# An mLSTM cell with a feed-forward block: loading the second chunk's output gates later and applying them in a step of their own

## The chip, the cores and the metric

The kernel runs on one core of a Trainium2 chip. The metric is the device time of one launch in microseconds (us). The core has five engines with a queue each: TensorE for matrix products (PE; its weight loads are shown as PEld), VectorE (DVE), ScalarE (ACT), GpSimd (POOL), and SyncE (SP), which here only issues loads and stores (DMAs). Each engine works through its own instructions in program order and waits on semaphores for what the others make.

## The reference

Two blocks follow one another. The first is an mLSTM cell with 4 batch rows, 8 heads, 768 steps and 40 numbers a head; the second is a feed-forward block with 2048 hidden features on the 3072 x 320 result.

```python
def _attn_ref(q, k, v, i_gate, f_gate, o_gate):
    ...
    for t in range(S):
        ...
        m_new = np.maximum(f_gate[:, :, t] + m, i_gate[:, :, t])
        f_stab = np.exp(f_gate[:, :, t] + m - m_new)
        i_stab = np.exp(i_gate[:, :, t] - m_new)
        m = m_new
        C = f_stab[:, :, None, None] * C + i_stab[:, :, None, None] * np.einsum('bhd,bhe->bhde', vt, kt)
        n = f_stab[:, :, None] * n + i_stab[:, :, None] * kt
        h_tilde = np.einsum('bhde,bhe->bhd', C, qt)
        nq = np.einsum('bhd,bhd->bh', n, qt)[:, :, None]
        denom = np.maximum(np.abs(nq), 1.0)
        o = 1.0 / (1.0 + np.exp(-o_gate[:, :, t]))
        y[:, :, t] = o * h_tilde / denom

def _moe_ref(x, w_in, w_out):
    h = x @ w_in
    g = h * np.cos(h)
    return g @ w_out
```

What matters here is the last line of the cell: an output is the value h_tilde, divided by denom and multiplied by the gate o. The two factors may be applied in either order and at different times, as long as both are in x before `x @ w_in` reads it.

## The kernel before, in words

**Cells and chunks.** The 768 steps are cut into 6 chunks of 128 steps. A cell is one chunk of one batch row, so there are 24 cells, numbered `n = 4 * chunk + row` from 0. A cell's product of scores and values is made by PE, normalised and gated, and written, turned so that features lie on partitions, into the tile `xT[chunk]`. This tile holds three blocks of features (two of 128, and one of 64 that is kept twice) for all 4 rows.

**The feed-forward slots.** Once the four cells of a chunk are in xT, their 512 tokens go through the feed-forward block in 8 slots, called `f2` from 0 to 7, with two 128-wide tiles of hidden features in each. `Up(c, f2)` issues the products with w_in into two banks of PSUM: eight matmuls on the two whole blocks (line 810) and four on the block of 64 (line 816). Then `near` (ACT, 824), `rest` (DVE, 827), `sin` (ACT, 832) and `gate` (DVE, 836) make h * cos(h). The pool `ps_u` has just the two banks of one Up, so the next Up starts only when the gates of the one before it have been made. `down(c, f2)` multiplies by w_out (848).

**What runs beside what.** `first_cells` makes cells 0 to 3. While chunk 0 goes through its slots, `first_parts(b)`, called for b = 0 to 3, makes cell `4 + b` of chunk 1 between the instructions of slots `2b` (i = 0) and `2b + 1` (i = 1). `both_parts` does the same for the later chunks. All is under a manual schedule: the order in the program is the order in every engine's queue. In `first_parts` the down product runs one slot behind, so that Up(0,7) is followed by down(0,6), then by Up(1,0), which is the first to read the xT of chunk 1.

**Weights.** w_in and w_out come in a 64-bit form. A piece is loaded into a tile `bits`, `take_apart` (two ACT instructions, lines 158 and 160) and `put_together` (three DVE instructions, 165 to 169, and one of POOL, 170) turn it into float32. w_in comes in four groups of three pieces, each group for two slots; the pool `pb` has four such tiles. w_out comes in eight pieces, one for each slot; `pc` has three tiles. `more` issues the next w_in piece's loads when a tile comes free, `next_out` does it for w_out.

**Output gates.** `load_o(c)` issues eight loads on SP into one raw tile. `sigmoid(c)` is three ACT instructions into `og`, of which there is one. ACT needs a table load (1.28 us each in this profile) when it changes between exponential, sigmoid and sine; `sin_next` loads the sine's table ahead of its use. For the cells of chunk 1, `turn_gate(n)` has DVE transpose a cell's gates into `oT` (line 524), and `normalize_turned(n)` makes 1/denom in `dt`, multiplies the values by the gates into `yt` (664), spreads 1/denom into `db` (668), and writes two blocks of xT (672). POOL makes the third block in `yt` (673), and `low_out(n)` has POOL issue two copies of it into xT (776). The pool `p1`, where oT, yt, db and the scaled queries qG lie, has one buffer for each tag: whoever writes such a tile next waits until all readers of the last content are done.

**Other names in the steps.** `scores`, `weigh`, `values` are a cell's products and the weighing by the decay E; `decay_exponents` masks E on POOL (438) and `decay` is its exponential on ACT (452). `turn_keys`/`keys_out` transpose keys on PE (502) and copy them by ACT (510), `turn_blocks` transposes queries on DVE (519), `scale_q` scales them on POOL (528), `seam_u`, `fade` and `state` carry the state. `hold(9)` issues nine dummy matmuls (1029).

Of the kernel before, what the change touches and what calls it, by code (L numbers as in the profile page):

```python
# [29 lines left out]
def kernel(  # L30
# [144 lines left out]
    def weights_in(f):  # L175
        for i in range(NK):
            src = [(slice(32 * a, 32 * a + 32), w_in_bits[D * (NK * a + i):D * (NK * a + i) + 32, ts(f, WP)]) for a in range(HP)]
            yield w_in_sb[:, i, ts(f, WP)], bits_in(WP, src, pb, WP)
        bits = pb.tile([128, WP, 2], I32, name="bits", tag="bits")
        for e in range(2):  # L180
            for a in range(2):
                nc.sync.dma_start(out=bits[64 * e:64 * e + 64, ts(a, 128)].rearrange("r n two -> r (n two)"), in_=w_in_last[e, 2 * f + a])
        yield w_in_l[:, ts(f, 2)].rearrange("p a n -> p (a n)"), bits
# [146 lines left out]
    def load_o(c, bs=range(B)):  # L330
        if c == 0:
            sig[c] = og.rearrange("q b k i -> q (b k i)")[:, 0:B * DM].rearrange("q (b h d) -> q b h d", b=B, h=H)
            for b in bs:
                nc.sync.dma_start(out=sig[c][:, b], in_=o_gate[b, :, ts(c, C)].rearrange("h t d -> t h d"))  # L334
            return
        raw_o[c] = p1.tile([128, B, 2 * C // 32, D], FP, name="o", tag="o")
        src = o_gate.rearrange("b (a g) (c t k) d -> a g c t b (k d)", g=2, k=C // 32, t=32)
        for a in range(HP):
            for g in range(2):
                dst = raw_o[c][32 * a:32 * a + 32].rearrange("t b (g k) d -> t g b (k d)", g=2)[:, g]  # L340
                nc.sync.dma_start(out=dst, in_=src[a, g, c])
# [306 lines left out]
    def normalize_turned(n):  # L648
# [24 lines left out]
        nc.gpsimd.tensor_tensor(out=yt[:, NK], in0=yt[:, NK], in1=db[:, NK], op=OP.mult)  # L673
        ys[n] = yt[:, NK]

    def normalize(n):
        c, b = divmod(n, B)
        hs = heads_of[n]
        dn = p2.tile([128, H], FP, name="dn", tag="dn")

        nc.vector.scalar_tensor_tensor(out=dn, in0=hs[:, :, D], scalar=-TWO_PI, in1=least, op0=OP.mult, op1=OP.max)
        nc.vector.scalar_tensor_tensor(out=dn, in0=hs[:, :, D], scalar=TWO_PI, in1=dn, op0=OP.mult, op1=OP.max)
        nc.vector.reciprocal(out=dn, in_=dn)
        y = p1.tile([128, 3 * C], FP, name="y", tag="yt")[:, 0:DM]
        t = p1.tile([128, 3 * C], FP, name="yo", tag="db")[:, 0:DM].rearrange("q (h d) -> q h d", h=H)
# [345 lines left out]
    def first_cells():  # L1031
# [68 lines left out]
        seam_out(0)  # L1100
        values(1)
        load_E(B + 1)
        load_o(1)
        scores(2)
        decay_exponents(3)
        normalize(1)
# [64 lines left out]
    def more():  # L1171
        for piece in feed[0]:
            pieces.append(piece)
            break

    def first_parts(b):
        n = B + b
        for i in range(2):
            f2 = 2 * b + i
            up = Up(0, f2)  # L1180
            if (b, i) == (0, 0):
                feed.append(piece for f in range(2, NF // 4) for piece in weights_in(f))
                more()
                load_E(n + 2)
                outs.append((2, weights_out(2)))
            if i == 0:
                scores(n)
                if b == 0:
                    seam_u(B - 1)
                    warm(3, psum_o())  # L1190
# [5 lines left out]
                if b > 0:  # L1196
# [6 lines left out]
                if b == 0:  # L1203
                    state(B - 1)
                    for e in range(2):
                        up.gate(e)
                    turn_blocks(n + 1)
                    next_out()
                    decay_exponents(n + 1)
                    sigmoid(1)  # L1210
                else:
                    for step in "gw" if b == 1 else "wg":
                        if step == "g":
                            for e in range(2):
                                up.gate(e)
                        elif pieces:
                            put_together(*pieces.pop(0))
                            more()
                    next_out()
                    decay(n + 1)  # L1220
                down_slot(0, f2)
                turn_gate(n)
                values(n)
                seam_u(n)
                fade(n)
                normalize_turned(n)
                low_out(n)
                if n == 2 * B - 1:
                    load_two(n + 3, "qk")
                if n > B + 1:  # L1230
                    load_E(n + 3)
                if b == B - 2:
                    load_o(2)
                sin_next()
                if b > 0:
                    if pieces:
                        take_apart(*pieces[0])
                        put_together(*pieces.pop(0))
                        more()
                        take_apart(*pieces[0])  # L1240
                    take_apart(*outs[0][1])
            else:
                if n == 2 * B - 1:
                    load_two(n + 3, "Kv")
                for e in range(2):
                    up.near(e)
                if b == 0:
                    for piece in pieces[0:2]:
                        take_apart(*piece)
                    put_together(*pieces.pop(0))  # L1250
                    more()
                for e in range(2):
                    up.rest(e)
                if b == 0:
                    put_together(*pieces.pop(0))
                    more()
                    load_two(n + 2, "Kv")
                else:
                    state(n)
# [6 lines left out]
                if b == 0:  # L1266
                    take_apart(*pieces[0])
                    take_apart(*outs[0][1])
                if b == 0:
                    state(n)  # L1270
                if pieces:
                    put_together(*pieces.pop(0))
                    if b == 0:
                        load_two(n + 2, "q")
                    more()
                if n == B + 1:
                    low_dimensions(n + 1)
                if b == 0:
                    decay(n + 1)
                else:  # L1280
                    turn_blocks(n + 1)
                    if b < B - 1:
                        turn_keys(n + 1)
                        keys_out(n + 1)
                next_out()
                scale_q(n + 1)
                down_slot(0, f2)
                if b == 0:
                    turn_keys(n + 1)
                    keys_out(n + 1)  # L1290
                    hold(9)
                if b == 1:
                    load_two(n + 3)
                if b < 2:
                    load_E(n + 3)
                if b == 1:
                    take_apart(*pieces[0])
                if b == B - 1:
                    weight_sums(0)

    def both_parts(c, b):
# [120 lines left out]
```

## Time and profile before

| | |
|---|---|
| median of 3 runs | 518.31 us (517.14 to 519.41) |
| the profiled execution's own time | 517.64 us |
| its span on the core | 515.9 us |
| first Up, Up(0,0), starts | 35.87 us |
| Up(0,2) starts | 59.34 us |
| Up(0,6) starts | 104.94 us |
| Up(1,0) starts | 126.10 us |
| granted TensorE clock | 1.00 throughout |

The page lists each engine's busy time. A timeline lists an engine's instructions in order: start and duration in us, engine, source line, operation, tile written and tiles read, and in brackets how long the engine was idle before it, and who released it. A wait list says which line waited for whom: us in total, how many times, the longest. In the listing of DMAs, "to landing" is the time from issue to arrival.

Over the 64 us from 66 to 130, PE is busy 63.27, DVE 55.38, ACT 46.38 and POOL 32.72 us, and the mean share of the 16 DMA engines is full; from 130 us on it is 0.32. In the 25 us from 35 to 60, PE is busy 21.98 us, the dummy matmuls among them.

### The profile page before, as it was taken

The numbers are of one execution on the slowest core, as the hardware profiler recorded it, in microseconds if no ns is written. First come the engines' busy times: TensorE is split into PE (matmuls) and PEld (weight loads), VectorE is DVE, ScalarE is ACT, GpSimd is POOL, SyncE is SP. The second block draws the span as 40 slices with busy tenths as digits, with TensorE's granted clock in tenths as the row PEclk, the third lists the DMA queues.
The fourth block names the chain that finished last, engine by engine and source line by source line (L and its number), as shares of the span: only waits on it lengthen the run. The fifth ranks groups of instructions, "written<-read, shape, count | busy, mean of one in ns | idle before, by whom it ended". The sixth has DMA issues, their size and how long they took to land.

```text
span 515.9 us, 13717 instructions
## 1 busy us (share of the span) xinstructions
PE 504.5 (98%) x5271; PEld 336.3 (65%) x5271; DVE 411.4 (80%) x965; ACT 316.1 (61%) x696; POOL 266.6 (52%) x434
## 2 busy tenths in 40 slices
PE   9999799999999999999999999999999999999996
PEld 5764455565576675775775775776776676666766
DVE  6687988987779888898878898878898778664636
ACT  4879897955876765965764965765854631323221
POOL 7627555644677778566455366455365333131211
PEclk9999999999999999999999999999999999999999
DMA  9997999999166466019574019475020000010001
GB/s 135 221 226 195 231 204 261 204 217 199 20 149 109 89 134 113 5 59 183 113 143 99 3 61 184 111 136 102 10 73 11 2 7 8 1 52 0 2 0 51
DMA packets 97265, 53.17 MB, mean 103 GB/s; under 512 B 62544, under 2 KB 89280, under 8 KB 97200
## 3 DMA queue, kind: packets, MB, share of 16 engines
q1 hardware_dynamic: 95408, 50.46, 47.7%
q0 software_dynamic: 1408, 1.48, 1.1%
q8 instruction: 41, 0.67, 0.6%
q10 hardware_dynamic: 384, 0.36, 0.2%
q14 instruction: 24, 0.20, 0.1%
HBM read 46.86 MB, written 4.11 MB: 99 GB/s over the span
## 4 chain that ended last, share of the span: by engine, by line
PE 80%; SPq 6%; ACT 5%; DVE 3%; DMA 3%; issue 2%; POOL 1%; ACTq 0%; DVEq 0%; POOLq 0%
PE pup L810 30%; PE acc L931 24%; PE pup L816 9%; PE po L848 4%; PE late L931 4%; PE vt L619 2%; SPq L359 2%; PE vt L630 2%; PE ps L550 2%; ACT E L452 1%; DMA bits<-in_moe_w_out_dram 1%; DVE n L827 1%; PE ps L554 1%; DMA G<-G_d 1%; SPq L334 1%
## 5 line engine op out<-in xcount | busy, mean ns | idle before, releaser
L810 PE MATMUL pup<-xT,w_in_sb 128*128 128x512 f32 x384 | 175.5, 600 | 2.1 <-DVE g L836 1.9
L824 ACT ACTIVATE n<-pup 128x512 int32<-128x512 f32 x96 | 53.7, 593 | 156.3 <-PE pup L816 100.9
L810 PEld LDWEIGHTS pup<-xT,w_in_sb 128*128 128x128 f32 x384 | 69.7, 190 | 87.9 <-issue 80.7
L827 DVE SCALAR_TENSOR_TENSOR n<-pup,n 128x512 f32<-128x512 f32 x96 | 63.3, 687 | 72.8 <-ACT n L824 70.7
L890 POOL TENSOR_TENSOR D<-g 128x128 f32<-128x128 f32 x40 | 20.0, 499 | 110.1 <-DVE g L836 103.0
L832 ACT ACTIVATE n<-n 128x512 f32<-128x512 f32 x96 | 59.3, 630 | 13.6 <-DVE n L827 13.6
L836 DVE SCALAR_TENSOR_TENSOR g<-pup,n 128x512 f32<-128x512 f32 x96 | 63.2, 686 | 3.1 <-ACT n L832 0.2
L931 PE MATMUL acc<-w_out_sb,g 128*128 128x160 f32 x320 | 58.5, 304 | 0.0
L931 PE MATMUL acc<-T,g 128*128 128x160 f32 x320 | 57.9, 301 | 0.1
L816 PE MATMUL pup<-xT,w_in_l 64*128 64x512 f32 x192 | 54.5, 642 | 0.1
L931 PEld LDWEIGHTS acc<-w_out_sb,g 128*128 128x128 f32 x320 | 47.8, 190 | 4.6 <-issue 3.7
L931 PEld LDWEIGHTS acc<-T,g 128*128 128x128 f32 x320 | 48.1, 190 | 3.2 <-issue 2.7
L452 ACT ACTIVATE E<-E,tab 128x64 f32<-128x64 f32 (+1 forms) x160 | 42.1, 345 | 1.3 <-POOL E L438 1.0
L848 PE MATMUL po<-w_out_sb,g 128*128 128x320 f32 x128 | 36.4, 437 | 0.4 <-POOL w_out_sb L170 0.4
L673 POOL TENSOR_TENSOR yt<-yt,db 128x128 f32<-128x128 f32 x20 | 11.0, 552 | 49.2 <-DVE db L668 49.2
L931 PE MATMUL acc<-T,S 128*128 128x160 f32 x160 | 34.9, 300 | 0.0
L528 POOL TENSOR_TENSOR qG<-t,G 128x512 f32<-128x512 f32 x20 | 25.4, 1272 | 12.4 <-DVE t L519 10.4
L848 PEld LDWEIGHTS po<-w_out_sb,g 128*128 128x128 f32 x128 | 23.7, 190 | 11.3 <-issue 1.5
L816 PEld LDWEIGHTS pup<-xT,w_in_l 64*128 64x128 f32 x192 | 14.7, 184 | 24.0 <-issue 20.6
L438 POOL TENSOR_SCALAR_AFFINE_SELECT E<-E 64x512 f32<-64x512 f32 (+1 forms) x38 | 27.5, 724 | 3.0 <-DVE E L435 1.9
L931 PE MATMUL acc<-w_out_sb,S 128*128 128x160 f32 x160 | 28.8, 299 | 0.0
L931 PEld LDWEIGHTS acc<-T,S 128*128 128x128 f32 x160 | 26.2, 190 | 2.7 <-issue 2.7
(214 smaller groups left out, 960.1 us busy)
## 6 DMA issues: line engine op xcount, KB each, us to landing
qr<-in_q_dram SPq DMA_DIRECT2D x36, 160.0 KB
G<-G_d SPq DMA_DIRECT2D x20, 256.0 KB
bits<-in_moe_w_out_dram SPq DMA_DIRECT2D x8, 640.0 KB
kr<-in_k_dram SPq DMA_DIRECT2D x32, 160.0 KB
bits<-in_moe_w_in_dram SPq DMA_DIRECT2D x32, 128.0 KB
E<-M_d SPq DMA_DIRECT2D x32, 128.0 KB
out_dram<-o_sb SPq DMA_DIRECT2D x22, 160.0 KB
o<-in_o_gate_dram SPq DMA_DIRECT2D x40, 80.0 KB
```

The lines of the kernel that those rows point to most:

```text
L438: nc.gpsimd.affine_select(out=E[x:x + w], in_=E[x:x + w], compare_op=OP.is_ge, fill=1.0e30, base=0, pattern=[[0, H], [1, w]], channel_mult ...
L452: nc.scalar.activation(out=Es[n][:, h], in_=Es[n][:, h], func=AF.Exp, scale=-1.0, bias=tab[:, c, 0, g:g + 1])
L528: nc.gpsimd.tensor_tensor(out=qG, in0=qkT[n][0], in1=Gs[n], op=OP.mult)
L810: nc.tensor.matmul(pu, w_in_sb[:, i, ts(2 * f2 + e, 128)], x(i), start=(i == 0 and not low_first), stop=(i == NK - 1 and low_first))
L816: nc.tensor.matmul(pu, w_in_l[r, f2], x(NK, r), start=low_first, stop=not low_first)
L824: nc.scalar.activation(out=self.n[e], in_=self.pu[e], func=AF.Copy, bias=0.25)
L827: nc.vector.scalar_tensor_tensor(out=self.n[e].bitcast(FP), in0=self.pu[e], scalar=0.25, in1=self.n[e], op0=OP.add, op1=OP.subtract)
L832: nc.scalar.activation(out=r, in_=r, func=AF.Sin, scale=TWO_PI_DOWN)
L836: nc.vector.scalar_tensor_tensor(out=g, in0=self.pu[e], scalar=TWO_PI, in1=self.n[e].bitcast(FP), op0=OP.mult, op1=OP.mult)
L848: nc.tensor.matmul(po[c][b], gs[c, f][:, ts(b, C)], w_out_sb[:, f], start=(f == 0), stop=(f == NF - 1))
L890: tt(out=D1, in0=G0[:, 1, 1], in1=G1[:, 1, 1], op=OP.add)
L931: nc.tensor.matmul(a, lhs, rhs, start=start, stop=stop)
```

## The change

It has three parts. `load_o(1)` moves from `first_cells`, where it stood ahead of w_in's second group on SP, to the end of b = 0, behind the loads of later weights, keys and queries and behind load_E(7). `sigmoid(1)` moves from b = 0 to b = 2, and `load_o(2)` stays behind it. As the gates of chunk 1 come later, cells 4, 5 and 6 are normalised without them by `normalize_first`, and gated later by `gate_late`, in b = 3: cell 4 before the gates of Up(0,6), cell 5 after down(0,5) has been issued, cell 6 at the end of the last slot's work. Cell 7 is made as before. Last, the work of b = 0 is written out in `first_slots` in another order: keys of cell 5 are turned after Up(0,2) has been issued (in b = 1, i = 0), all three pieces of w_in's second group are taken apart before `near` of Up(0,1), and the dummy matmuls are left out.

```diff
+    def normalize_first(n):
+        c, b = divmod(n, B)
+        dn = p2.tile([128, C], FP, name="dt", tag="dt")
+        va, vb = heads_of[n]
+        nc.vector.tensor_scalar(out=dn, in0=va[:, 1], scalar1=-TWO_PI, scalar2=TWO_PI, op0=OP.mult, op1=OP.max)
+        nc.vector.scalar_tensor_tensor(out=dn, in0=va[:, 1], scalar=TWO_PI, in1=dn, op0=OP.mult, op1=OP.max)
+        nc.vector.reciprocal(out=dn, in_=dn)
+        db = p1.tile([128, 3, C], FP, name="db", tag="db")
+        for i, mask in enumerate(([FROM0] * 32, [FROM1] * 32, [FROM0] * 16 + [FROM1] * 16)):
+            nc.vector.stream_shuffle(out=db[:, i], in_=dn, mask=mask)
+        if b == 0:
+            xT[c] = p2.tile([128, NK + 1, B, C], FP, name="xT", tag="xT")
+        nc.vector.tensor_tensor(out=xT[c][:, 0:3:2, b], in0=va, in1=db[:, 0:3:2], op=OP.mult)
+        nc.vector.tensor_tensor(out=xT[c][:, 1, b], in0=vb, in1=db[:, 1], op=OP.mult)
+
+    def gate_late(n):
+        c, b = divmod(n, B)
+        turn_gate(n)
+        yt = p1.tile([128, 3, C], FP, name="yt", tag="yt")
+        nc.gpsimd.tensor_tensor(out=yt[:, NK], in0=xT[c][:, NK, b], in1=oTs[n][:, NK], op=OP.mult)
+        ys[n] = yt[:, NK]
+        low_out(n)
+        nc.gpsimd.tensor_tensor(out=xT[c][:, 0:NK, b], in0=xT[c][:, 0:NK, b], in1=oTs[n][:, 0:NK], op=OP.mult)
...
         load_E(B + 1)
-        load_o(1)
         scores(2)
...
+    def first_slots():
+        n = B
+        up = Up(0, 0)
...
+        take_apart(*outs[0][1])
+        state(B - 1)
+        for e in range(2):
+            up.gate(e)
+        turn_blocks(n + 1)
+        next_out()
+        decay_exponents(n + 1)
+        for piece in pieces[0:2]:
+            take_apart(*piece)
+        join()
+        values(n)
+        seam_u(n)
+        fade(n)
+        join()
+        up = Up(0, 1)
+        take_apart(*pieces[0])
+        for e in range(2):
+            up.near(e)
+        for e in range(2):
+            up.rest(e)
+        join()
+        for e in range(2):
+            up.sin(e)
+            up.gate(e)
+        load_two(n + 2, "Kv")
+        load_two(n + 2, "q")
+        take_apart(*outs[0][1])
+        weigh_k(n + 1)
+        odd_values(n + 1)
+        scale_q(n + 1)
+        decay(n + 1)
+        normalize_first(n)
+        next_out()
+        state(n)
+        down_slot(0, 1)
+        load_E(n + 3)
+        load_o(1)
...
             if i == 0:
+                if b == 1:
+                    turn_keys(n)
+                    keys_out(n)
                 scores(n)
...
+                if b < B - 1:
+                    decay_exponents(n + 1)
+                else:
+                    gate_late(B)
                     decay_exponents(n + 1)
...
-                    decay_exponents(n + 1)
-                    sigmoid(1)
...
                 down_slot(0, f2)
-                turn_gate(n)
+                if b == B - 1:
+                    gate_late(B + 1)
+                    turn_gate(n)
                 values(n)
                 seam_u(n)
                 fade(n)
-                normalize_turned(n)
-                low_out(n)
+                if b == B - 1:
+                    normalize_turned(n)
+                    low_out(n)
+                else:
+                    normalize_first(n)
...
                 if b == B - 2:
+                    sigmoid(1)
                     load_o(2)
...
-                if b == 0:
-                    turn_keys(n + 1)
-                    keys_out(n + 1)
-                    hold(9)
...
                 if b == B - 1:
+                    gate_late(B + 2)
                     weight_sums(0)
```

`join` is `put_together` of the first waiting w_in piece, followed by `more`. `B` is 4, `NK` is 2.

More of the change, by code (lines that the diff above doesn't have):

```diff
@@ L1174, in more, with join @@
             break
+    def join():
+        if pieces:
+            put_together(*pieces.pop(0))
+            more()
+    def first_slots():
+        n = B
+        up = Up(0, 0)
+        feed.append(piece for f in range(2, NF // 4) for piece in weights_in(f))
+        more()
+        load_E(n + 2)
+        outs.append((2, weights_out(2)))
+        scores(n)
+        seam_u(B - 1)
+        warm(3, psum_o())
+        for e in range(2):
+            up.near(e)
+        for e in range(2):
+            up.rest(e)
+        weigh(n)
+        for e in range(2):
[16 more added lines that the diff above has]
+        take_apart(*pieces[0])
+        for e in range(2):
+            up.near(e)
+        for e in range(2):
+            up.rest(e)
+        join()
+        for e in range(2):
+            up.sin(e)
+            up.gate(e)
[12 more added lines that the diff above has]
+        load_o(1)
     def first_parts(b):
         n = B + b
+        if b == 0:
+            first_slots()
+            return
         for i in range(2):
@@ L1180, in first_parts @@
             up = Up(0, f2)
[L1181 to L1185, printed above, removed]
             if i == 0:
+                if b == 1:
+                    turn_keys(n)
+                    keys_out(n)
                 scores(n)
-                if b == 0:
-                    seam_u(B - 1)
-                    warm(3, psum_o())
                 for e in range(2):
@@ L1195, in first_parts @@
                 weigh(n)
-                if b > 0:
+                if b < B - 1:
+                    decay_exponents(n + 1)
+                else:
+                    gate_late(B)
                     decay_exponents(n + 1)
@@ L1202, in first_parts @@
                 take_apart(*outs[0][1])
[L1203 to L1208, printed above, removed]
-                    decay_exponents(n + 1)
-                    sigmoid(1)
[L1211 to L1220, printed above, removed]
+                for step in "gw" if b == 1 else "wg":
+                    if step == "g":
+                        for e in range(2):
+                            up.gate(e)
+                    else:
+                        join()
+                next_out()
+                decay(n + 1)
                 down_slot(0, f2)
-                turn_gate(n)
+                if b == B - 1:
+                    gate_late(B + 1)
+                    turn_gate(n)
                 values(n)
@@ L1225, in first_parts @@
                 fade(n)
-                normalize_turned(n)
-                low_out(n)
+                if b == B - 1:
+                    normalize_turned(n)
+                    low_out(n)
+                else:
+                    normalize_first(n)
                 if n == 2 * B - 1:
@@ L1232, in first_parts @@
                 if b == B - 2:
+                    sigmoid(1)
                     load_o(2)
                 sin_next()
[L1235 to L1241, printed above, removed]
+                if pieces:
+                    take_apart(*pieces[0])
+                    join()
+                    take_apart(*pieces[0])
+                take_apart(*outs[0][1])
             else:
@@ L1246, in first_parts @@
                     up.near(e)
[L1247 to L1251, printed above, removed]
                 for e in range(2):
                     up.rest(e)
[L1254 to L1259, printed above, removed]
+                state(n)
                 for e in range(2):
@@ L1265, in first_parts @@
                 odd_values(n + 1)
[L1266 to L1276, printed above, removed]
-                    low_dimensions(n + 1)
[L1278 to L1282, printed above, removed]
-                        turn_keys(n + 1)
-                        keys_out(n + 1)
+                join()
+                if b == 1:
+                    low_dimensions(n + 1)
+                turn_blocks(n + 1)
+                if b < B - 1:
+                    turn_keys(n + 1)
+                    keys_out(n + 1)
                 next_out()
@@ L1287, in first_parts @@
                 down_slot(0, f2)
-                if b == 0:
-                    turn_keys(n + 1)
-                    keys_out(n + 1)
-                    hold(9)
                 if b == 1:
                     load_two(n + 3)
-                if b < 2:
                     load_E(n + 3)
-                if b == 1:
                     take_apart(*pieces[0])
                 if b == B - 1:
+                    gate_late(B + 2)
                     weight_sums(0)
```

## The prediction

> **What bounds the kernel now.** First the page's busy shares, then the waits of PE after 130 us:
>
> ```profile
> PE 504.5 (98%) x5271; PEld 336.3 (65%) x5271; DVE 411.4 (80%) x965; ACT 316.1 (61%) x696; POOL 266.6 (52%) x434
> ```
>
> ```profile
> PE pup L810 <- DVE g L836: 0.2, 1, 0.2
> ```
>
> TensorE (PE) sets the end. From 130 us to the end it waited for other engines 0.2 us in all, so nothing there can absorb a delay, and what PE loses or wins earlier moves the end one for one. What it can win lies in the first slots. SP's timeline, then PE's (start, duration, line; idle before it and its releaser in brackets):
>
> ```profile
> 34.58 9.86 SPq L341 DMA_DIRECT2D o<-in_o_gate_dram  x8
> 44.61 4.87 SPq L147 DMA_DIRECT2D bits<-in_moe_w_in_dram  x8
> 49.58 2.65 SPq L182 DMA_DIRECT2D bits<-in_moe_w_in_dram  x4
> 52.27 0.45 SPq L364 DMA_DIRECT2D ks<-in_k_dram  x1
> ```
>
> ```profile
> 50.57 4.57 PE L848 MATMUL po<-w_out_sb,g 128*128 128x320 f32 x16
> 56.07 0.63 PE L502 MATMUL pt<-ident,ks 128*128 128x128 f32 x4 [0.92 <-DMA ks<-in_k_dram]
> 56.54 1.40 PE L1029 MATMUL po<-nil 128*128 128x320 bf16 x9
> 59.34 3.67 PE L810 MATMUL pup<-xT,w_in_sb 128*128 128x512 f32 x8 [1.40 <-DVE g L836]
> ```
>
> The eight o_gate loads hold SP's queue for 9.86 us; w_in's second group stands behind them. PE ends its first down product at 55.05 and starts Up(0,2) at 59.34. Between lie the keys' load, nine dummy matmuls and the gates of Up(0,1), which on VectorE (DVE) stand behind the late weights. Those 4.29 us are all that the head can give; two later waits of PE, 0.33 and 0.40 us at 82 and 88 us, are the only other ones before 130.
>
> **Where the change puts a wait.** The seam to the second chunk: PE's, DVE's and GpSimd's (POOL's) timelines, then the landing of the copy that low_out(7) issues.
>
> ```profile
> 121.69 4.58 PE L848 MATMUL po<-w_out_sb,g 128*128 128x320 f32 x16
> 126.10 3.60 PE L810 MATMUL pup<-xT,w_in_sb 128*128 128x512 f32 x8
> ```
>
> ```profile
> 122.48 1.29 DVE L827 SCALAR_TENSOR_TENSOR n<-pup,n 128x512 f32<-128x512 f32 x2 [2.72 <-ACT n L824]
> ...
> 128.68 0.83 DVE L169 SCALAR_TENSOR_TENSOR w_out_sb<-bits,w_out_sb 128x640 int32<-128x640 int32 x1
> ```
>
> ```profile
> 111.09 1.37 POOL L438 TENSOR_SCALAR_AFFINE_SELECT E<-E 64x512 f32<-64x512 f32 x2
> ...
> 119.52 0.55 POOL L673 TENSOR_TENSOR yt<-yt,db 128x128 f32<-128x128 f32 x1 [1.16 <-DVE db L668]
> 120.37 1.10 POOL L776 DMA_DIRECT2D xT<-yt  x2 [0.29 <-POOL yt L673]
> ...
> 129.64 1.56 POOL L170 TENSOR_TENSOR w_out_sb<-w_out_sb,bits 128x640 int32<-128x640 int32 x1 [6.86 <-DMA ks<-in_k_dram]
> 131.15 1.28 POOL L528 TENSOR_TENSOR qG<-t,G 128x512 f32<-128x512 f32 x1
> ```
>
> ```profile
> DMA to landing us min/median/max: 5.3/5.6/5.8
> ```
>
> Up(1,0) starts at 126.10, with only one down product after Up(0,7). It reads xT of all four cells. In the new order the last gate_late, cell 6's, stands on POOL behind scale_q(8), which ends at 132.43: after Up(1,0) has begun in the old run.
>
> **The change, part by part.** Times are on the clock of the old run.
>
> *load_o(1) behind load_E(7).* The eight loads leave SP's place at 34.58. DMA was full there (share 1.0 from 34 to 42 us), so about 5 of the 9.86 us were back pressure that w_in's loads inherit: the load of the next o_gate chunk at 108.30 took 5.80 us for the same eight. So w_in's group, keys and w_out(1) come about 5 us earlier: the last w_in piece is issued by 47.1 and landed by 51 (issue to landing 2.7 to 3.8 us in this stretch). On ScalarE (ACT) it now stands before near of Up(0,1): 51 + 0.76 for take_apart, then 3.3 us from near to the first gate (79.38 to 82.7 in slot b=1): 55.1. Up(0,2) can start at 55.1, right behind the down product: **-4.2 us**, the dummies and the later keys in it. The turn of keys now costs PE 0.6 us (copy by ACT before scores), in place of the 1.02 us wait for the same copy at 65.15. Bounds: -4.9 (with half of the two later waits more) and 0, if the last piece lands 4 us later.
>
> *sigmoid(1) from slot b=0 to b=2, i=0.* It is three instructions and a table: 1.28 + 0.97 + 0.51 = 2.8 us. In b=0 it lay in ACT's queue before Up(0,1)'s near; now it lies before near of Up(0,5), and ACT was full there: from the sine's end at 90.15 to near at 100.30 only 0.18 us was idle. Near goes to 102.9, the first gate from 103.21 to 105.55; it ends 0.65 later, at 106.2, where Up(0,6) wanted its bank at 104.94. **+1.3 us**, and +0.2 for the w_out(5) product behind the same DVE queue: **+1.5**; bounds 0 and 2.6. Its raw loads are long there; load_o(2) waits for it on SP, and the loads behind that are wanted only after 125 us.
>
> *normalize_first in place of normalize_turned for cells 4 to 6.* DVE loses one 128x256 product (0.41) and the turn of the gates (0.9) in each of three slots, POOL its 0.55 and two DMA issues (1.10). PE does not wait for them there: nothing. If the cover of PE's own work were gone they would be worth 1.3 us a slot.
>
> *gate_late three times in b=3.* Each is a turn (0.75 from start to start on DVE), and on POOL 0.55, 0.29 idle, two issues 1.10, and a 128x256 product that no row has: between the 0.55 of 128x128 and the 1.04 of 128x512 (L457); I take 0.75, as a 128x256 add of w_in_l took. oT and yt have one buffer each, so each step waits for the last one's readers, the copy included.
> - Cell 4: its turn stands before Up(0,6)'s gates, ready 113.6. POOL: yt 114.15, second copy issued 115.0, xT 116.3. The mask of E(8) goes from 111.09 to 116.3, w_out(6) ends 119.25.
> - Cell 5: its yt waits for that copy, 115.0 + 5.2 = 120.2 (that between 4.7 and 5.8, the rows of the first chunk). yt 120.75, second copy issued 121.6, xT 122.9.
> - The turn for cell 7 waits on DVE for that xT: 122.9. Behind it stands normalize_turned(7), whose first write of yt waits for the copy: 121.6 + 5.2 = 126.8; its ten instructions from there take 2.5 (117.22 to 119.75): 129.3.
> - Behind that on DVE is rest of Up(0,7), at 122.48 before. From there to the end of w_out(7) is 7.03 us in the old run, without idle time: 136.3. POOL: w_out(7) to 137.95, scale_q(8) to 139.2.
> - Cell 6: yt 139.75, copies 140.05 to 141.15, xT 141.9. Up(1,0) starts there: 141.95 - 126.10 = **+15.9 us**.
> Bounds: with landings of 1.7 us, as in the chunks that load little, yt of cell 5 follows w_out(6) at 119.25, normalize_turned(7) starts writing at 123.25, 3.55 earlier: 12.3. Upper: landings of 5.8 and 1.0 for the product, 17.4.
>
> The Trainium skill ("DMA: Bandwidth & Descriptors", "Anatomy of one DMA") gives a GpSimd DMA a fixed cost of about 2 us; by it the stall would be 12.3 and not 15.9. The rows differ: about 5 us while the loads run and 1.7 us later, so I keep the row.
>
> *PE after the stop.* The only matmuls in the trace that follow a long idle time are the first: nine of 128x512 took 4.02 us, while three later took 0.82, or 2.08 for nine at their pitch. So a cold start loses 1.9 us. No gap over 1.4 us stands inside the run, so the bounds are 0 and 1.9; a stop of 16 us is nearest to the start: **+1.9**.
>
> The Trainium skill ("TensorE: Matmul & The Clock Gate", "What's actually happening") has the array at half clock after an idle window of some 3.4 us, until as long a busy one. Half of that, 1.7 us, is an estimate from that page; the sum would be 532.5. No run here shows it in mid-kernel yet.
>
> **Sum.** The profiled execution took 517.64 us (span 515.9, 1.7 around it; the median of the runs is 518.31, 0.1% above). 517.64 - 4.2 + 1.5 + 15.9 + 1.9 = 532.7 us.
>
> **Rivals.**
> - Short landings: SP's loads are through before 115 us and the copies land in 1.7 us. For it: SP gets some 5 us ahead. Against it: DMA was full until 130 us, and the bytes stay the same. 517.64 - 4.2 + 1.5 + 12.3 + 1.9 = 529.1.
> - Only the last link binds: the waits of cells 5 and 7 are covered, and cell 6 is gated right behind scale_q(8) at 132.43: 132.43 + 0.55 + 0.29 + 1.10 + 0.75 = 135.1, a stall of 9.0: 525.8. Against it: the one-buffer tiles.
> - The first edit doesn't do what it says: the weights stay late because back pressure, not the o_gate loads, held them. -0.5 in place of -4.2: 536.4. For it: DMA share 1.0 from 34 to 42 us. Against it: 0.6 from 42 to 54.
> - Not slower: the seam holds, cell 6 gated before PE has ended its down product. It decides from the point where xT of cell 6 is written by 126.1; then 517.64 - 4.2 + 1.5 = 514.9. Against it: Up(0,7) ends at 121.76, and DVE alone needs until 129.5 to come to that turn.
>
> **How the numbers follow.** Forecast 0.58, short landings 0.14, last link 0.12, weights late 0.10, not slower 0.06. The range from 524 to 537.5 us holds all but the last and the outer bounds. A difference under 0.5% (2.6 us) can't be told from none; 514.9 lies on that edge, so its 0.06 is halved: faster 0.03, same 0.03, slower 0.94.
>
> **What would show it.** Up(0,2) right behind the first down product near 55; ACT's near of Up(0,5) late by 2.6; on DVE two idle stretches before the turn for cell 7 and before its yt; PE idle for some 16 us ahead of Up(1,0), released by POOL, with the first matmuls behind it at twice their time. I am wrong if PE idles under 5 us there, or if the head gives back more than 6.

## The result, and the profile after

The changed kernel takes 537.83 us (median of 6 runs, 535.63 to 540.45), the kernel before 517.90 us in the runs beside it (6 runs, 517.11 to 521.18). The ratio is 1.038, with a 95% interval of 1.034 to 1.042: slower. The forecast was 532.7, its range 524 to 537.5; the median lies 0.3 us above the range. The profiled execution of the changed kernel took 535.63 us, the shortest of the six; its span is 533.9 us, 18.0 more than before.

The first thing to look at is whether PE works more or waits more. The page's busy shares of the changed kernel, then the waits of PE between 35 and 200 us (waiting line, releaser: us in total, times, longest):

```profile
PE 504.3 (94%) x5262; PEld 335.4 (63%) x5262; DVE 413.3 (77%) x962; ACT 314.7 (59%) x694; POOL 269.7 (51%) x437
```

```profile
PE pup L834 <- POOL xT L698: 14.6, 1, 14.6
PE pup L834 <- DVE g L860: 4.2, 3, 2.5
PE pt L502 <- DMA ks<-in_k_dram: 1.1, 1, 1.1
```

PE is as busy as before (504.3 us against 504.5), so the added time is waiting. One wait holds 14.6 of the 18.0 us, and POOL releases it: line 698 is the last instruction of `gate_late`. PE's timeline has the places (start, duration, line; idle before it and its releaser in brackets). Up is now lines 834 and 840, the down product 872.

```profile
57.61 3.67 PE L834 MATMUL pup<-xT,w_in_sb 128*128 128x512 f32 x8 [2.45 <-DVE g L860]
...
105.22 3.70 PE L834 MATMUL pup<-xT,w_in_sb 128*128 128x512 f32 x8 [1.54 <-DVE g L860]
...
117.82 3.70 PE L834 MATMUL pup<-xT,w_in_sb 128*128 128x512 f32 x8
...
122.51 4.57 PE L872 MATMUL po<-w_out_sb,g 128*128 128x320 f32 x16
141.67 5.41 PE L834 MATMUL pup<-xT,w_in_sb 128*128 128x512 f32 x8 [14.58 <-POOL xT L698]
147.01 1.13 PE L840 MATMUL pup<-xT,w_in_l 64*128 64x512 f32 x4
```

Set against the old starts, these lines give the balance, in us:

| place | before | after | difference | by the forecast |
|---|---|---|---|---|
| Up(0,2) starts | 59.34 | 57.61 | -1.73 | -4.2 |
| Up(0,5) starts | 95.44 | 94.03 | -1.41 | -4.2 |
| Up(0,6) starts | 104.94 | 105.22 | +0.28 | -2.9 |
| Up(0,7) starts | 117.00 | 117.82 | +0.82 | -2.7 |
| Up(1,0) starts | 126.10 | 141.67 | +15.57 | +13.2 |
| its block of 64 starts | 129.63 | 147.01 | +17.38 | +15.1 |
| end of the span | 515.9 | 533.9 | +18.0 | +15.1 |

**The seam** shows the forecast's two links on DVE. Here are its turns of gates (524), the first write of `yt` for cell 7 (664), and the work behind it:

```profile
117.64 0.87 DVE L524 STREAM_TRANSPOSE oT<-og 128x384 f32<-128x384 f32 x1
123.20 0.92 DVE L524 STREAM_TRANSPOSE oT<-og 128x384 f32<-128x384 f32 x1 [4.69 <-POOL xT L698]
...
126.72 0.42 DVE L664 TENSOR_TENSOR yt<-vt,oT 128x256 f32<-128x256 f32 x1 [2.15 <-DMA xT<-yt]
...
129.18 1.28 DVE L851 SCALAR_TENSOR_TENSOR n<-pup,n 128x512 f32<-128x512 f32 x2
...
135.32 0.83 DVE L169 SCALAR_TENSOR_TENSOR w_out_sb<-bits,w_out_sb 128x640 int32<-128x640 int32 x1
```

The turn for cell 7 waits 4.69 us until cell 5 no longer reads the one `oT`; the write of `yt` waits 2.15 us more, until cell 5's copy has left the one `yt`. Only at 129.18 can DVE take `rest` of Up(0,7), whose product has been there since 122.6 and whose `near` ACT began at 123.78. POOL follows:

```profile
119.03 1.56 POOL L170 TENSOR_TENSOR w_out_sb<-w_out_sb,bits 128x640 int32<-128x640 int32 x1
120.55 0.46 POOL L695 TENSOR_TENSOR yt<-xT,oT 128x128 f32<-128x128 f32 x1
...
136.28 1.56 POOL L170 TENSOR_TENSOR w_out_sb<-w_out_sb,bits 128x640 int32<-128x640 int32 x1 [4.00 <-issue]
137.79 1.26 POOL L528 TENSOR_TENSOR qG<-t,G 128x512 f32<-128x512 f32 x1
139.01 0.46 POOL L695 TENSOR_TENSOR yt<-xT,oT 128x128 f32<-128x128 f32 x1
139.76 1.10 POOL L800 DMA_DIRECT2D xT<-yt  x2 [0.29 <-POOL yt L695]
140.88 0.73 POOL L698 TENSOR_TENSOR xT<-xT,oT 128x256 f32<-128x256 f32 x1
```

Cell 6 is gated last, behind w_out(7) and the scaled queries, and Up(1,0) starts when line 698 ends.

**The clock.** Windows of the changed kernel: stretch, length, busy us and instructions of PE, PEld, DVE, ACT and POOL, then PEclk, the granted clock, DMA share and GB/s.

```profile
128.00:130.00 2.00, 0.00 (x0) 0.00 (x0) 1.96 (x10) 0.10 (x1) 0.68 (x2) 1.00 1.37 149
130.00:132.00 2.00, 0.00 (x0) 0.00 (x0) 1.96 (x7) 2.00 (x6) 1.98 (x4) 0.87 1.50 153
132.00:134.00 2.00, 0.00 (x0) 0.00 (x0) 2.00 (x3) 0.19 (x1) 0.28 (x2) 0.50 0.46 68
134.00:142.00 8.00, 0.33 (x1) 0.33 (x2) 2.85 (x5) 0.00 (x0) 5.41 (x7) 0.50 0.02 8
142.00:144.00 2.00, 2.00 (x3) 0.85 (x3) 0.00 (x0) 0.00 (x0) 1.76 (x5) 0.50 0.00 0
144.00:146.00 2.00, 2.00 (x4) 0.72 (x3) 0.00 (x0) 0.00 (x0) 1.15 (x2) 0.71 0.00 0
```

A mean of 0.87 over 2 us is 0.52 us at half clock, so it fell at 131.5, 4.4 us after PE had stopped at 127.1. A mean of 0.71 is 1.16 us at half: it rose at 145.2. Of that time 3.5 us lie in Up(1,0), whose eight matmuls took 5.41 us in place of 3.60. In the table, that is the step of 1.81 us between the start of Up(1,0) and that of its block of 64.

**The head.** DVE's weights of w_in's second group, and POOL's work at the same time:

```profile
48.33 1.68 DVE L167 TENSOR_SCALAR w_in_sb<-w_in_sb 128x512 int32<-128x512 int32 x1
50.05 1.46 DVE L169 SCALAR_TENSOR_TENSOR w_in_sb<-bits,w_in_sb 128x512 int32<-128x512 int32 x1
...
51.87 1.40 DVE L167 TENSOR_SCALAR w_in_sb<-w_in_sb 128x512 int32<-128x512 int32 x1
53.31 1.20 DVE L169 SCALAR_TENSOR_TENSOR w_in_sb<-bits,w_in_sb 128x512 int32<-128x512 int32 x1
...
56.78 1.28 DVE L860 SCALAR_TENSOR_TENSOR g<-pup,n 128x512 f32<-128x512 f32 x2
```

```profile
48.09 1.63 POOL L170 TENSOR_TENSOR w_out_sb<-w_out_sb,bits 128x640 int32<-128x640 int32 x1 [3.77 <-ACT bits L160]
49.68 1.27 POOL L438 TENSOR_SCALAR_AFFINE_SELECT E<-E 128x1024 f32<-128x1024 f32 x1
51.64 1.34 POOL L170 TENSOR_TENSOR w_in_sb<-w_in_sb,bits 128x512 int32<-128x512 int32 x1 [0.68 <-ACT n L848]
52.94 1.02 POOL L736 TENSOR_TENSOR st<-st,fades 128x384 f32<-128x384 f32 x1
```

Compare ends, not starts. The two L167 end at 50.01 and 53.27, 0.29 us after a POOL instruction each (49.72 and 52.98); the two L169 end at 51.51 and 54.51, 0.56 and 0.55 us after one (50.95 and 53.96). Alone, these instructions take 0.43 and 0.69 us. Ends that keep so constant a distance from POOL's speak for instructions that run when POOL has finished: what the trace shows as their duration is then mostly waiting. Experiment e7 tests it.

### The profile page after: what moved, and what is told of

Same layout as the page of the kernel before. It is cut to its first block, busy times and chain, and to the rows that moved or that the text cites. A ratio compares the mean times of both kernels' runs of the same rounds, so it can differ in the third digit from the quotient of the medians.

```text
span 533.9 us, 13696 instructions
## 1 busy us (share of the span) xinstructions
PE 504.3 (94%) x5262; PEld 335.4 (63%) x5262; DVE 413.3 (77%) x962; ACT 314.7 (59%) x694; POOL 269.7 (51%) x437
## 4 chain that ended last, share of the span: by engine, by line
PE 71%; DMA 10%; SPq 7%; ACT 5%; issue 2%; DVE 2%; POOL 2%; ACTq 0%; POOLq 0%; DVEq 0%
PE pup L834 28%; PE acc L955 24%; PE pup L840 8%; PE late L955 4%; DMA bits<-in_moe_w_in_dram 3%; DMA bits<-in_moe_w_out_dram 3%; PE vt L619 2%; DMA ks<-in_k_dram 2%; SPq L359 2%; PE vt L630 2%; PE ps L550 2%; SPq L147 1%; DMA E<-M_d 1%; SPq L334 1%; SPq L182 1%
## 5 line engine op out<-in xcount | busy, mean ns | idle before, releaser
L834 PE MATMUL pup<-xT,w_in_sb 128*128 128x512 f32 x384 | 177.6, 605 | 19.5 <-POOL xT L698 14.6
L856 ACT ACTIVATE n<-n 128x512 f32<-128x512 f32 x96 | 59.3, 630 | 20.0 <-DVE n L851 19.9
L955 PE MATMUL acc<-T,g 128*128 128x160 f32 x320 | 57.9, 301 | 0.1
L673 POOL TENSOR_TENSOR yt<-yt,db 128x128 f32<-128x128 f32 x17 | 9.4, 553 | 49.3 <-DVE db L668 49.3
L840 PEld LDWEIGHTS pup<-xT,w_in_l 64*128 64x128 f32 x192 | 14.6, 184 | 23.4 <-issue 21.0
```

The costliest lines, as they stand in the source:

```text
L834: nc.tensor.matmul(pu, w_in_sb[:, i, ts(2 * f2 + e, 128)], x(i), start=(i == 0 and not low_first), stop=(i == NK - 1 and low_first))
L840: nc.tensor.matmul(pu, w_in_l[r, f2], x(NK, r), start=low_first, stop=not low_first)
L856: nc.scalar.activation(out=r, in_=r, func=AF.Sin, scale=TWO_PI_DOWN)
L955: nc.tensor.matmul(a, lhs, rhs, start=start, stop=stop)
```

## The experiments

Each kernel was run beside the kernel before on the same chip. That one had a median of 516.77 us (13 runs) beside the first four and of 516.91 (27 runs) beside the last four. All eight start from the changed kernel; in those that edit `gate_late`, line numbers behind it are 3 higher.

### e1: the gates in time

The first question is whether the seam is the whole loss. The late gating moves ahead, to where nothing waits: cells 4 and 5 right behind `sigmoid(1)`, cell 6 at the start of the last slot pair. So that the steps don't wait for one another, even cells use two constant tiles that are idle then, in place of `oT` and `yt`; one of them, `ending`, is set back to zero afterwards.

```diff
-        turn_gate(n)
-        yt = p1.tile([128, 3, C], FP, name="yt", tag="yt")
+        late = "" if n % 2 else "l"
+        turn_gate(n, late)
+        yt = wall.rearrange("p h t -> p (h t)").bitcast(FP)[:, 0:C] if late else p1.tile([128, 3, C], FP, name="yt", tag="yt")[:, NK]
...
+        if n == B + 2:
+            nc.gpsimd.memset(ending, 0.0)
...
-                    gate_late(B)
                     decay_exponents(n + 1)
+                    gate_late(B + 2)
...
-                    gate_late(B + 1)
...
                     sigmoid(1)
+                    gate_late(B)
+                    gate_late(B + 1)
...
-                    gate_late(B + 2)
```

> The changed kernel, with cells 4 and 5 gated right behind the sigmoid in b=2 and cell 6 behind the mask of E(8) at the start of b=3, in tiles of their own. My theory (the loss is the stop ahead of Up(1,0), 14.6 us, and the cold clock behind it): no stop at the seam, granted clock 1.00, 518 to 520 us, because the head's gain (1.4) and the sigmoid's cost (1.7) about cancel. Rival (the loss only moves: gating 3 cells late costs the same work on DVE and POOL wherever it stands): PE waits in b=2 and b=3 instead, 525 us or more.

Measured: 519.97 us (518.50 to 521.97, 10 runs), ratio 1.005 (1.003 to 1.007). PE's first Up after the head, and Up(1,0):

```profile
57.39 5.37 PE L837 MATMUL pup<-xT,w_in_sb 128*128 128x512 f32 x8 [2.46 <-DVE g L863]
...
128.52 3.60 PE L837 MATMUL pup<-xT,w_in_sb 128*128 128x512 f32 x8
```

Up(1,0) follows the down product without a stop and at full clock. So the late gating at the seam is the loss. What remains is some 3 us. The head ought to bring a gain, but what it wins at the start of Up(0,2) (1.95 us) is lost again there: the eight matmuls took 5.37 us in place of 3.67. A stop of 2.46 us had let the clock fall here too:

```profile
56.00:58.00 2.00, 0.61 (x2) 0.40 (x3) 1.97 (x5) 1.98 (x4) 1.22 (x2) 0.98 0.99 188
58.00:60.00 2.00, 2.00 (x4) 0.86 (x3) 1.89 (x9) 1.99 (x6) 1.92 (x3) 0.50 1.03 267
60.00:62.00 2.00, 2.00 (x4) 0.76 (x3) 1.90 (x6) 1.25 (x5) 0.00 (x0) 0.66 1.08 391
```

By the same arithmetic it was at half from 57.9 to 61.4. The rest is lost in b = 2 and 3: Up(0,6) starts 1.23 us later than before, behind a stop of 1.12 us for DVE's gates, and Up(0,7) 2.42 us later, since the down product ahead of it waits 1.01 us for a piece of w_out on POOL. The four runs with a mean clock of 0.998 or more took 518.50 to 518.92, the six at 0.995 to 0.997 took 519.92 to 521.97.

### e2: dummy matmuls into the stop

`hold(90)` before Up(1,0) issues 90 of the dummy matmuls that the old head had nine of. They are meant to fill the stop and change nothing else.

```diff
                     gate_late(B + 2)
+                    hold(90)
                     weight_sums(0)
```

> The changed kernel with 90 dummy matmuls (12 us) ahead of Up(1,0), to keep PE busy while it waits. My theory (half clock after the stop): Up(1,0) starts at the same moment, near 141.7, its eight matmuls take 3.6 us and not 5.4, clock 1.00; 533.5 to 534.5 us, and the runs lie within 2 us of each other. Rival (the spread of the runs, 535.6 to 540.5, is not the clock): median stays at 537 to 538 with the same spread.

Measured: 536.31 us (533.68 to 537.28, 4 runs), ratio 1.036 (1.032 to 1.040). In its profile the dummies ran from 127.91 to 140.47. PE then stood still for 3.87 us, the clock was half from 144, and Up(1,0) took 5.17 us from 144.34. Up(0,2) was cold too (5.37 us). So this run does not answer its question: 90 dummies were too few, and there was a second stop that it left open. The one run with a mean clock of 0.998 took 533.68. In e5 both stops are filled.

### e3: tiles of their own

Here `gate_late` stays where the change put it, but never uses the `oT` and `yt` of p1. This removes the two waits on DVE at 123.20 and 126.72; all it adds is one reset of `ending` on POOL, behind the last gating.

```diff
-        turn_gate(n)
-        yt = p1.tile([128, 3, C], FP, name="yt", tag="yt")
+        late = "l"
+        turn_gate(n, late)
+        yt = wall.rearrange("p h t -> p (h t)").bitcast(FP)[:, 0:C] if late else p1.tile([128, 3, C], FP, name="yt", tag="yt")[:, NK]
```

> The changed kernel, its order unchanged, but gate_late has an oT and a yt of its own, so cell 7 waits for neither on DVE. My theory (waits on one-buffer tiles, 4.7 and 2.2 us on DVE, are part of the chain; near of Up(0,7) at 123.8 then sets rest): Up(1,0) starts some 5 us earlier, a stop of 9 to 10 us, 529 to 533 us with the cold clock. Rival 1 (the last link alone sets the end): nothing changes, 536 to 538. Rival 2 (these waits are the whole of the stop): 519 to 522.

Measured: 531.81 us (531.26 to 533.23, 4 runs), ratio 1.029 (1.026 to 1.032).

```profile
136.53 6.63 PE L837 MATMUL pup<-xT,w_in_sb 128*128 128x512 f32 x8 [9.77 <-POOL xT L699]
```

The stop is 9.77 us in place of 14.58. About a third of it came from the single buffers; the other two thirds come from the place alone, behind w_out(7) and `scale_q(8)`, which follow `rest` of Up(0,7) (124.04 here, behind ACT's `near`). The rival "only the last link binds" had 9.0 us for this and described this kernel, not the changed one. The stop is shorter, but the matmuls behind it lose more: 6.63 us in place of 3.60, where the change took 5.41. The clock was at half from 128.8 to 142.5. Why is worked out below, with the clock.

### e4: the old head

The first slot pair, `load_o(1)` and `sigmoid(1)` go back to their old places; only the late gating is left of the change.

```diff
         load_E(B + 1)
+        load_o(1)
...
-        for piece in pieces[0:2]:
-            take_apart(*piece)
-        join()
-        values(n)
...
+                sigmoid(1)
+                down_slot(0, f2)
+                values(n)
...
+                turn_keys(n + 1)
+                keys_out(n + 1)
+                hold(9)
...
-                    sigmoid(1)
                     load_o(2)
```

> The changed kernel with the first slot pair, load_o(1) and sigmoid(1) as they were before; only normalize_first and gate_late remain of the change. By the two traces the new head gains 1.4 us up to Up(0,5) and the sigmoid loses 1.7 at Up(0,6), so this is within 1.5 us of the changed kernel: 536 to 539. Rival (the new head is worth its 4.2 us and something later ate it): 539.5 or more.

Measured: 537.07 us (534.47 to 540.17, 4 runs), ratio 1.039 (1.034 to 1.044), against 1.038 for the whole change. Up(0,2) starts at 58.55, Up(0,6) at 104.74 without a stop, Up(0,7) at 116.80, and Up(1,0) at 141.62 after a stop of 15.56 us. Taken together the earlier loads, the new order and the moved sigmoid are worth nothing that can be measured; with the late gating alone the loss is the same. The spread of the four runs goes with the clock: at mean clocks of 0.987, 0.981, 0.979 and 0.976 they took 534.47, 537.06, 537.09 and 540.17.

### e5: both stops kept warm

`hold(14)` before Up(0,2) and `hold(102)` before Up(1,0), so that neither stop leaves PE idle for long.

```diff
             f2 = 2 * b + i
+            if f2 == 2:
+                hold(14)
             up = Up(0, f2)
...
                     gate_late(B + 2)
+                    hold(102)
```

> The changed kernel with dummy matmuls in both of its stops: 14 ahead of Up(0,2) (1.9 us of the 2.45) and 102 ahead of Up(1,0) (14.2 us; the 90 of the run before left 3.9 us idle and the clock fell). My theory (the clock halves after either stop, in some executions after the first too): granted clock 1.00, both Ups' eight matmuls at 3.6 to 3.7 us, all runs within 2 us of each other near 533.5 to 534.5. Rival (the clock has nothing to do with the 2.2 us between the median, 537.8, and the profiled 535.6): 536 to 538 with the old spread.

Measured: 533.36 us (533.16 to 534.41, 4 runs), ratio 1.032 (1.029 to 1.034).

```profile
57.47 3.67 PE L834 MATMUL pup<-xT,w_in_sb 128*128 128x512 f32 x8 [0.52 <-DVE g L860]
...
126.27 14.21 PE L1053 MATMUL po<-nil 128*128 128x320 bf16 x102
142.98 3.70 PE L834 MATMUL pup<-xT,w_in_sb 128*128 128x512 f32 x8 [2.50 <-POOL xT L698]
```

Every run has a mean clock of 0.998 or more, and the spread falls from 4.8 us to 1.25. Against the kernel before beside it, the loss is 16.5 us (533.36 - 516.91), against 19.9 for the change (537.83 - 517.90): so the half clock costs some 3.5 us of the median, and the intervals of the two ratios leave this open by about 2.5 us either way. In the profiled execution, the slowest of the four, the copy of cell 5 landed later than in the change (6.8 us after its issue in place of 4.7), and Up(1,0) started 1.3 us later; whether the other three share this is not seen.

### e6: e1 with a warm head

```diff
             f2 = 2 * b + i
+            if f2 == 2:
+                hold(14)
```

> The kernel that gates in time, with 14 dummy matmuls in the stop ahead of Up(0,2). My theory (the 2.45 us stop, which the old head filled with 9 dummies, lets the clock fall: Up(0,2) took 5.4 us): clock 1.00, Up(0,2) back at 3.7, 518 to 518.6 us where the kernel without them took 519.97. Rival (the clock falls for another reason, PE's light load around 40 to 56 us): no change, 520.

Measured: 520.40 us (519.10 to 521.32, 8 runs), ratio 1.006 (1.004 to 1.008). The clock did what was expected (0.998 to 1.00 in all runs, Up(0,2) 3.67 us), the time did not: e1's runs at a clock of 1.00 took 518.50 to 518.92, these 519.10 and more. In the profile Up(0,5) starts 1.73 us earlier than before. The gain is gone by Up(0,7): PE stops 1.13 us ahead of Up(0,6) for DVE's gates and 1.00 us ahead of the down product for a piece of w_out on POOL. Up(1,0) starts 0.7 us later than before and the span ends 1.6 later, so about half of what is left is lost behind the seam. What sets that half was not settled.

### e7: POOL's work out of DVE's way

e1, with the mask of E(5) and the fade of cell 4 on POOL moved behind the last piece of w_in's second group.

```diff
         next_out()
-        decay_exponents(n + 1)
         for piece in pieces[0:2]:
             take_apart(*piece)
         join()
         values(n)
         seam_u(n)
-        fade(n)
         join()
...
         join()
+        decay_exponents(n + 1)
+        fade(n)
```

> The kernel that gates in time, with POOL's mask of E(5) and fade(4) moved behind the last piece of w_in's second group. My theory (in the head DVE's put_together instructions stretch from 0.43 and 0.69 us to 1.2 to 1.7 while POOL works at the same time): the two 169s that overlapped those two fall to 0.7, Up(0,2) starts 1.0 to 1.5 us earlier, its stop is near 1.2 us and the clock stays at 1.00; 516.5 to 518.5 us. Rival (DVE is slow there because of the loads or of ACT, not POOL): durations and start of Up(0,2) unchanged, 519.5 to 520.5.

Measured: 518.89 us (517.18 to 521.27, 10 runs), ratio 1.003 (1.001 to 1.005). DVE's same four instructions:

```profile
48.15 1.68 DVE L167 TENSOR_SCALAR w_in_sb<-w_in_sb 128x512 int32<-128x512 int32 x1
49.86 0.69 DVE L169 SCALAR_TENSOR_TENSOR w_in_sb<-bits,w_in_sb 128x512 int32<-128x512 int32 x1
...
50.92 1.40 DVE L167 TENSOR_SCALAR w_in_sb<-w_in_sb 128x512 int32<-128x512 int32 x1
52.36 0.69 DVE L169 SCALAR_TENSOR_TENSOR w_in_sb<-bits,w_in_sb 128x512 int32<-128x512 int32 x1
```

The two whose overlap was removed are back at 0.69 us; the two that still overlap line 170 keep 1.68 and 1.40. Up(0,2) starts at 56.17 in place of 57.39, 1.22 us earlier, where the two gave back 1.28 (0.77 and 0.51). That is POOL's doing, and neither the loads' nor ACT's. For the other two, which overlap line 170 in both runs, the cause rests on their ends alone. The median came out above what was expected, since PE lost 1.70 us ahead of cell 5's scores, where it had been 0.68 in e1 (the trace names `near` of Up(0,2) on ACT as the releaser; the copy of the turned keys stands ahead of that), and the clock still fell in some runs: four at 0.998 and more took 517.18 to 517.95, the other six 518.88 and more. In the profiled one it was at half from 63.5 to 66.9, behind that new stop, and the scores took 1.84 us in place of 1.16.

### e8: what is good in all of them

e7, with `sigmoid(1)` at the end of b = 2; cell 4 gated behind the mask of E(8), cell 5 where the change has it, cell 6 right behind `low_out(7)`; all three in tiles of their own; the keys and values of cell 6 loaded before the third `join`; and `hold(6)` before Up(0,2).

```diff
-                    gate_late(B)
                     decay_exponents(n + 1)
+                    gate_late(B)
...
                     low_out(n)
+                    gate_late(B + 2)
...
-                    sigmoid(1)
-                    load_o(2)
...
+                if b == B - 2:
+                    sigmoid(1)
+                    sin_next()
+                    load_o(2)
```

> The one before, with sigmoid(1) moved to the end of b=2, where ACT idled 5.3 us ahead of near of Up(0,6); cells 4 and 5 gated in the first half of b=3, cell 6 behind normalize_turned(7), all in tiles of their own; keys and values of cell 6 loaded ahead of the next w_in piece; 6 dummy matmuls ahead of Up(0,2). My theory: the 1.1 to 1.5 us stop ahead of Up(0,6) goes, Up(1,0) starts some 2.5 to 3 us before 126.1; 514 to 515.5 us, faster than the kernel before by 0.2 to 0.5%. Rival (the gates again come too late for Up(1,0)): a stop at the seam, 518 or more.

Measured: 516.13 us (515.48 to 517.70, 12 runs), ratio 0.999 (0.997 to 1.0003) to the kernel before; 514 to 515.5 had been expected. Up(1,0) starts at 123.99, 2.1 us earlier than before, and the profiled span is 513.7, 2.2 shorter. But the profiled execution is among the fastest of the twelve, and over the runs the kernel cannot be told from the one before. Up(0,6) and Up(0,7) start 3.09 us earlier than before; 0.82 of it goes to a stop ahead of Up(1,0), released by line 699 (698 in the change): the rival's stop is there, though small. What the earlier loads can give is about the size of what one execution differs from the next.

## Why the prediction was right in its mechanism and too low in its time

**The seam: right.** The chain went as forecast, link for link: the turn for cell 7 at 123.20 (forecast 122.9), `yt` at 126.72 (126.8), `rest` of Up(0,7) at 129.18 (129.3), POOL's `scale_q` done at 139.05 (139.2), Up(1,0) at 141.67 (141.95). That these moments agree to a few tenths is partly luck. They were worked out on the clock of the old run, and by the forecast's own head and sigmoid all of them would have come 2.7 us earlier; Up(0,7) came 0.82 us later. Measured from Up(0,7) on, as the sum needs it, the stop added 14.75 us: 141.67 - 117.82, less the old 126.10 - 117.00. The forecast had 15.9, inside its bounds. One link had another cause than was said: cell 5's `yt` at 120.55 waited for w_out(6) on POOL, not for cell 4's copy, which landed in 3.1 us and not in 5.2. Cell 5's copy took 4.7. So neither copy took the 5.2 us that was assumed, and neither the 1.7 of "short landings"; cell 4's was short enough to drop out, and cell 5's was on the path.

**The head: the step that failed.** The forecast for Up(0,2) was 55.1, from three terms. Two held: the loads came early (the last piece was there at 50.24, where 51 was the forecast), and ACT's `near` of Up(0,1) started at 51.04 where 51.76 had been worked out. The third, "3.3 us from near to the first gate (79.38 to 82.7 in slot b=1)", is wrong: in the new order DVE still puts together the second and third piece between the two, and POOL works beside it. The four stretched instructions of the first two pieces cost 3.5 us more than alone (1.25, 0.77, 0.97, 0.51), and the first gate came at 56.78 to 57.4. From `near` to the end of that gate it was 6.4 us in place of 3.3. Up(0,2) started at 57.61, 2.5 us after the forecast; another 0.3 us was lost by Up(0,5). The trace of before already had the rows against it: there lines 167 and 169 took 1.33 and 1.19 us on the smaller piece of 128x256 (36.21 and 37.58, beside POOL's lines 170 and 438), where 0.29 and 0.43 are its times alone. The 3.3 us, from a slot without such an overlap, had no room for them. The Trainium skill ("SBUF — State Buffer", "Who interferes with whom") says that a DVE instruction with two inputs in SBUF contends with a GpSimd instruction that reads SBUF, as does one in a mode that uses both ports, and that the one issued later is blocked until the other has ended. The ends in this trace, 0.29 and 0.55 us after POOL's, agree, and for line 169, which has two inputs, e7 shows it by taking the overlap away. Whether line 167, with one input, runs in such a mode is not seen in these views. The rival "the first edit doesn't do what it says" came nearer in size (-0.5 us, with -1.41 measured up to Up(0,5)) for the wrong reason: the weights were early, DVE was not.

**The sigmoid: right place, a little small.** ACT's table loads and gates stand before `near` of Up(0,5), as forecast:

```profile
94.46 1.28 ACT L350 ACT_TABLE_LOAD   x1
...
97.24 1.28 ACT L1184 ACT_TABLE_LOAD   x1
...
101.79 1.05 ACT L848 ACTIVATE n<-pup 128x512 int32<-128x512 f32 x2
```

Near came at 101.79, 2.9 us later relative to Up(0,5) than before (forecast 2.6). From Up(0,5) to Up(0,7) the kernel lost 2.23 us, where 1.5 had been taken; the bounds went to 2.6.

**The clock: right in the profile, too small for the median.** The term of 1.9 us was 1.81 in the profiled execution. The forecast took one execution's price as if every execution paid it. Mean clocks of the six runs are 0.987 in the profiled one and 0.979 to 0.982 in the others; (1 - clock) x 2 x span is the time at half, 13.9 us there and 22.6 us at 0.979. The runs of 540.3 and 540.5 us go with the latter: 8.7 us more at half can cost half of that at most, 4.4, and they took 4.7 and 4.8 more. e5 supports it: with the clock held, most of the spread and some 3.5 us of the median are gone. In which stretches the other executions ran at half is not seen, as only one was profiled; in e1 and e2 it was at the head as well, behind the stop of some 2.45 us that took the place of nine dummies.

The Trainium skill ("TensorE: Matmul & The Clock Gate", "What's actually happening") has half clock set in after an idle window of some 3.4 us that runs freely. The length agrees. The clock was at half for 3.41 us at a time in e1, e2 (twice) and e7, and for 13.65 us, four times that, in the change, e3 and e4; the two falls of e2, at 58.58 and 143.92, lie 25.0 times 3.41 us apart. That the whole window must be idle is not what these traces show. Here are stretches of 3.41 us, counted in whole steps from a fall in the same trace:

| run | stretch | PE busy in it, us | clock behind it |
|---|---|---|---|
| e1, the stop of 2.46 us | 54.52 to 57.93 | 0.95 | half |
| e2, the stop of 2.43 us | 55.17 to 58.58 | 1.18 | half |
| e3, start of its long stop | 125.39 to 128.80 | 1.38 | half |
| e7, the stop of 1.70 us | 60.08 to 63.49 | 1.71 | half |
| e3, a stop of 2.44 us | 53.71 to 57.12 | 1.73 | full |
| the change, first part of 2.45 us | 52.99 to 56.40 | 2.17 | full |
| the change, second part | 56.40 to 59.81 | 2.20 | full |

So a stop counts by how much of one such stretch it leaves idle, and not by its length alone. In e1 nearly the whole stop fell into one stretch, and Up(0,2) lost 1.70 us; in the profile of the change a boundary cut the stop in two, and nothing was lost. The line lies near half of the stretch, but busy time alone does not draw it: at the end of the spans of e2 and e4, stretches with 1.51 and 1.55 us of work were not followed by half clock. Full clock came back at the end of the first stretch that was busy for 2.90 us (e4) or more; 2.51 were not enough in e3. There PE resumed at 136.53, early in a stretch that ended at 139.04, and had to work through the next one as well: hence 3.03 us lost behind a shorter stop.

**The sum.** Head 2.8 us too good by Up(0,5), sigmoid 0.7 too small, seam 1.15 and cold start 0.1 too large, and 0.6 lost behind: 2.9 us in all, from 532.7 to the 535.6 of the profiled execution. That this one lies inside the range is owed in part to the seam, whose error runs against the others. The median lies 2.2 us higher still and out of the range; e5 speaks for the clock of the other executions as the cause. With either the head or the spread allowed for, the median would have been inside: the upper end held all mechanisms, but no spread between executions.

## What to carry to other kernels

Before work is moved off an early stage, follow it to the instruction that reads its result: here three late gatings landed on the two engines that PE next waits for, in tiles with one buffer. When the order on two engines changes, price an instruction by the rows in which the other engine is as busy as it will be, not by the shortest rows. A stop that is new on PE can cost more than its length (up to 3.0 us more here, and nothing behind one stop of 2.45), and not the same in every execution, so the range needs room on that side.

## What the runs showed of the hardware

- Two of DVE's `put_together` instructions (lines 167 and 169), of 128x512, took 0.43 and 0.69 us alone, and up to 1.68 and 1.46 us beside POOL, ending a constant 0.29 and 0.55 us after POOL's instruction.
- The granted clock fell 2.0 us (e3) to 4.8 us (e4) after PE had stopped, and in e1, e2 and e7 0.3 to 1.2 us after PE was at work again. It came back 2.9 us (e4) to 5.9 us (e3) after PE had resumed. In every profile with such a fall the time at half was, around a stop, 3.41 us or four times that. A stop of about 2.45 us cost 1.7 us or nothing, by where it lay in that pattern.
- The landing of one copy of POOL's, with the same bytes in the same place of the program, took 4.7 us in the change, 5.4 in e4 and 6.8 in e5 while loads ran, and 1.7 at 140 us, when none did.
